# Regrouping the float16 correction matmuls of a fused convolution and feed-forward kernel: one block of sixteen per four steps instead of one of eight per two

## The chip, the cores and the metric

The kernel runs on one core of one Trainium2 chip. The metric is the device time of one execution in microseconds (us). TensorE does the matmuls (PE in the rows; its weight loads are PEld), VectorE (DVE) and ScalarE (ACT) do the elementwise work, GpSimd (POOL) and SyncE (SP) issue transfers.

## The reference

A dynamic convolution with softmax weights over seven taps, then a feed-forward layer with a squared ReLU, over 32768 rows of 192:

```python
w = softmax(weight_gen, axis=-1)                      # (8, 4096, 8 heads, 7 taps)
x = einsum('bshk,bskhg->bshg', w, windows_of(x_pad))  # (32768, 192) after the reshape
h = x @ w_in                                          # (192, 2048)
g = np.maximum(h, 0.0) ** 2
out = g @ w_out                                       # (2048, 192), float32
```

## The kernel before

The rows are cut into 64 chunks of 512. Chunk `c` goes through eight steps `j`, and each step makes two blocks of 128 of the 2048 hidden columns. Float32 accuracy comes from splitting each number into a high part and a rest, so a product is made of several matmuls.

A step of the main loop writes, for PE: first `mm1(c, j)` (L537), 18 matmuls that multiply the chunk's input by `W` into two PSUM banks `ph`: six with `xh` (the input's high part, three pieces of two), six with `xl` (its rest, three pieces of two), six with `xh` again. Then the second product of the step that lies two steps back (`LAG`): `mm2_scaled(c2, j2)`, twelve matmuls with `gh` and `V` at L618. So the second products of a chunk's steps 6 and 7 stand in the next chunk's steps 0 and 1. All these use half of the array's rows each and run in pairs.

For chunks 6 to 62 the rest of `g`, called `gl`, is kept in float16 (five tiles of the pool, and three places inside the tile `du`; `V16`, the float16 weights, lies in `du` too). Its products with `V16` stand in two places of `mm2_scaled`: 32 small ones at L627, all in the chunk's last second product (`j2` = 7), and 32 at L635, four for each step. The line that this case is about says when those at L635 are written: before, in every second step, for that step and the one before it. Nothing reads the sums `acc` before the chunk's last one.

ACT makes from `ph` the ReLU (L554), the square (L561) and the cast to `gh` (L565); DVE makes `gl` (L574) one step later in its own order. When a chunk's last second product is done, `sum_turned` copies two accumulators out on ACT (L668) and adds two on DVE (L670): first `acc2` and `acc3`, which L627 ends, then, after the two casts of the step, `acc0` and `acc1`, which L635 ends.

Between these, DVE makes the convolution of the chunk after next, and the rest `xl` of the next chunk's input, three pieces at L447: two in step 6, the third in step 7. It is read by `mm1` of the next chunk's step 0. In every even chunk from 4 to 60 ACT also measures the next group's inputs in step 2 (`measure`, L279).

The order on each engine is the order in which the program writes it (a manual schedule); there is no planner that weighs costs.

Of the kernel before, what the change touches and what calls it, by code (L numbers as in the profile page):

```python
# [30 lines left out]
def kernel(  # L31
# [81 lines left out]
    def two_halves(t):  # L113
        return t.rearrange("p (i m) -> p m i", i=2)
# [493 lines left out]
    def mm2_scaled(c, j):  # L608
        if j == 0:
            accs[c] = [ps_o.tile([P, N], F32, name=f"acc{t}") for t in range(4)]  # L610
        acc, last = accs[c], j == NJ - 1
        gs = [ghs.pop((c, 2 * j + i)) for i in range(2)]

        def whole(i, b, e):
            fb = 2 * j + i
            for h in range(2):
                rows = slice(h * D1, (h + 1) * D1)
                nc.tensor.matmul(acc[b + h], V[rows, fb, e:e + P], two_halves(gs[i][rows]), start=fb == 0 and e < 2 * P, stop=False)  # L618

        for i, b, e in [(i, 2, P) for i in range(2)] + [(i, 0, e) for i in range(2) for e in (0, 2 * P)]:  # L620
            whole(i, b, e)
        if last:
            for k in range(NJ):
                for h in range(2):
                    for i in range(2):
                        rows = slice(h * D1, (h + 1) * D1)
                        nc.tensor.matmul(  # L627
                            acc[2 + h][i * D1:(i + 1) * D1], V16[rows, 2 * k + i, P:D], gls[c, k][rows, i],
                            start=False, stop=k == NJ - 1, tile_position=(h * D1, i * D1),
                        )  # L630
        for k in (j - 1, j) if j % 2 else ():
            for i in range(2):
                for h in range(2):
                    rows = slice(h * D1, (h + 1) * D1)
                    nc.tensor.matmul(acc[h], V16[rows, 2 * k + i, 0:P], gls[c, k][rows, i], start=False, stop=k == NJ - 1 and i == 1)  # L635
        if last:
            for k in range(NJ):
                del gls[c, k]

    def mm2_turned(c, fb):  # L640
        if is_scaled(c):
            if fb % 2 == 0:
                mm2_scaled(c, fb // 2)
            return
        if fb == 0:
            accs[c] = [ps_o.tile([P, N], F32, name=f"acc{t}") for t in range(4)]
        gh, gl = ghs.pop((c, fb)), gls.pop((c, fb))
        j, i = divmod(fb, 2)
        first, last = fb == 0, fb == NF - 1
        A, B = [(0, 0, gh), (0, 0, gl), (0, 1, gh)], [(2, None, gh), (2, None, gl)]  # L650
        seq = B + A if last or first else A + B
        for n, (b, q, g) in enumerate(seq):
            k = sum(1 for m in seq[:n] if m[0] == b)
            for h in range(2):
                rows = slice(h * D1, (h + 1) * D1)
                w = V[rows, fb, P:2 * P] if q is None else V[rows, fb, 2 * P * q:2 * P * q + P]
                fl = dict(start=first and k == 0, stop=last and k == (2 if b == 0 else 1))
                nc.tensor.matmul(accs[c][b + h], w, (two_halves if is_turned(c) else two_streams)(g[rows]), **fl)  # L658
# [346 lines left out]
```

## Time and profile before

| | |
|---|---|
| median of 3 runs | 2046.72 us (2046.34 to 2046.79) |
| the profiled execution, its own time | 2046.86 us |
| its span, first to last instruction | 2045.1 us |
| PE busy | 2038.0 us, 100% of the span |
| DVE busy | 1873.8 us, 92% |
| ACT busy | 1836.8 us, 90% |
| granted TensorE clock | 1.0 |

The profiled execution is 0.14 us above the median, and 1.76 us of its time lie around the span. Busy time counts instructions under way. Matmuls overlap, so a busy PE need not be at its peak; what matters is how far apart the matmuls start.

### The profile page before, as it was taken

To read this page: it belongs to the slowest core of one execution; us is meant where nothing else is said; L and a number is where in the kernel's file an instruction comes from. 1 tells how busy PE (TensorE), PEld (TensorE's weight loads), DVE (VectorE), ACT (ScalarE), POOL (GpSimd) and SP (SyncE) were. 2 spreads that over 40 slices of the span, in tenths; PEclk is the share of its full clock that TensorE was granted. 3 is DMA by queue.
4 is the path that set the end of the run, shared out by engine and by line. 5 is a ranking of instruction groups with operands and counts; after the bars stand their busy time and mean duration, and the time that the engine had idled before them with its cause. 6 is when DMAs were issued, how large, how long until landed. Compare 5 with 4: busy or idle time off the path is not lost.

```text
span 2045.1 us, 49783 instructions
## 1 busy us (share of the span) xinstructions
PE 2038.0 (100%) x19484; PEld 1637.7 (80%) x19484; DVE 1873.8 (92%) x3009; ACT 1836.8 (90%) x3551; POOL 226.5 (11%) x371
## 2 busy tenths in 40 slices
PE   9999999999999999999999999999999999999999
PEld 8888887877777877777777778787777787877778
DVE  8999999999999999999999999999999999999985
ACT  8989998989989989889899899998898998999986
POOL 0100111011110111101111101111011111011110
PEclk9999999999999999999999999999999999999999
DMA  8433453433444434534345344344453453443422
GB/s 232 92 82 69 97 108 85 104 77 90 105 99 95 93 76 100 111 88 104 71 93 109 93 99 81 84 105 107 92 105 67 95 112 87 103 78 89 105 57 46
DMA packets 346341, 193.44 MB, mean 95 GB/s; under 512 B 216032, under 2 KB 320992, under 8 KB 342264
## 3 DMA queue, kind: packets, MB, share of 16 engines
q1 hardware_dynamic: 324136, 156.00, 32.4%
q0 software_dynamic: 21968, 34.25, 10.2%
q8 instruction: 152, 2.49, 0.5%
q14 instruction: 85, 0.70, 0.1%
HBM read 57.77 MB, written 25.17 MB: 41 GB/s over the span
## 4 chain that ended last, share of the span: by engine, by line
PE 94%; DVE 3%; ACT 1%; DMA 0%; issue 0%; DVEq 0%; SPq 0%
PE ph L537 46%; PE acc L618 28%; PE acc L635 10%; PE acc L627 5%; PE acc L658 3%; PE acc L595 1%; DVE pr L401 0%; DVE gl L577 0%; DVE pr L414 0%; DVE gl L574 0%; DMA pr<-pr 0%; ACT rg L561 0%; DVE xl L447 0%; ACT rg L554 0%; DVE xr L507 0%
## 5 line engine op out<-in xcount | busy, mean ns | idle before, releaser
L537 PE MATMUL ph<-xh,W 64*128 64x512 f32 x6096 | 868.9, 390 | 0.0
L618 PE MATMUL acc<-gh,V 64*128 64x512 f32 x5472 | 665.1, 376 | 0.0
L537 PEld LDWEIGHTS ph<-xh,W 64*128 64x128 f32 x6096 | 580.3, 186 | 101.6 <-DVE W L239 0.3
L554 ACT ACTIVATE rg<-ph 128x512 f32<-128x512 f32 x992 | 541.7, 603 | 123.1 <-PE ph L537 115.1
L561 ACT ACTIVATE rg<-rg 128x512 f32<-128x512 f32 x1007 | 583.9, 640 | 0.2
L565 ACT CAST gh<-rg 128x512 fp32r<-128x512 f32 x1008 | 578.7, 631 | 3.0 <-PE acc L595 3.0
L618 PEld LDWEIGHTS acc<-gh,V 64*128 64x128 f32 x5472 | 518.0, 186 | 72.5
L537 PE MATMUL ph<-xl,W 64*128 64x512 f32 x3048 | 415.1, 376 | 1.1 <-DVE xl L447 0.8
L401 DVE TENSOR_TENSOR pr<-xt,wt 128x768 f32<-128x768 f32 x440 | 412.3, 949 | 2.3
L574 DVE TENSOR_TENSOR gl<-rg,gh 128x512 f16<-128x512 f32 x570 | 388.7, 737 | 2.1 <-ACT gh L565 2.1
L537 PEld LDWEIGHTS ph<-xl,W 64*128 64x128 f32 x3048 | 290.5, 186 | 42.6 <-DVE xl L447 2.1
L414 DVE TENSOR_TENSOR pr<-pr 128x768 f32<-128x768 f32 x309 | 294.3, 952 | 4.2
L574 DVE TENSOR_TENSOR du<-rg,gh 128x512 f16<-128x512 f32 x342 | 231.3, 730 | 4.0 <-ACT gh L565 4.0
L670 DVE TENSOR_TENSOR raw<-acc,raw 128x512 f32<-128x512 f32 x124 | 85.3, 691 | 123.3 <-ACT raw L668 123.3
L672 POOL DMA_DIRECT2D raw<-raw x62 | 51.6, 832 | 1141.0 <-DVE raw L670 1103.8
L635 PEld LDWEIGHTS <-du 64*128 64x128 f16 x1824 | 70.8, 95 | 118.1 <-issue 64.5
L635 PE MATMUL acc<-gl,du 64*128 64x512 f16 x1140 | 152.8, 379 | 0.0
L668 ACT COPY raw<-acc 128x512 f32<-128x512 f32 x124 | 72.1, 587 | 60.3 <-PE acc L627 60.3
L294 POOL DMA_DIRECT2D x_out<-x_fac x232 | 112.0, 491 | 110.1 <-DVE x_fac L291 104.3
L447 DVE TENSOR_TENSOR xl<-xT,xh 128x512 fp32r<-128x512 f32 x186 | 120.8, 679 | 2.8 <-ACT xh L444 2.8
L419 POOL DMA_DIRECT2D pr<-pr x63 | 57.1, 906 | 496.6 <-DVE pr L401 362.3
L444 ACT CAST xh<-xT 128x512 fp32r<-128x512 f32 x186 | 110.1, 636 | 0.4 <-issue 0.3
(129 smaller groups left out, 1267.4 us busy)
## 6 DMA issues: line engine op xcount, KB each, us to landing
xT<-xr SPq DMA_DIRECT2D x496, 96.0 KB
xt<-in_x_dram SPq DMA_DIRECT2D x30, 1344.0 KB
out_dram<-o_sb SPq DMA_DIRECT2D x254, 96.0 KB
pr<-pr POOLq DMA_DIRECT2D x63, 384.0 KB, 4.9
o_sb<-raw SPq DMA_DIRECT2D x372, 64.0 KB
raw<-raw POOLq DMA_DIRECT2D x62, 128.0 KB, 4.9
wt<-in_weight_gen_dram SPq DMA_DIRECT2D x31, 224.0 KB
x_out<-x_fac POOLq DMA_DIRECT2D x232, 0.1 KB, 2.1
```

The source lines that it names most:

```text
L294: nc.gpsimd.dma_start(out=fo[b * P // n:(b + 1) * P // n], in_=f[b::n])
L401: tt(out=dst, in0=src, in1=wf[:, t0 * H:t1 * H, k:k + 1].broadcast_to([P, m, G]), op=ALU.mult)
L414: tt(out=prs[k0], in0=prs[k0], in1=prs.pop(k), op=ALU.add)
L444: nc.scalar.copy(parts["h"][:, k, n], src[k][:, n])
L447: tt(out=parts["l"][:, k, n], in0=src[k][:, n], in1=parts["h"][:, k, n].bitcast(F32), op=ALU.subtract)
L537: nc.tensor.matmul(two[i], w, order(xx[rows, k]), start=(n == 0), stop=(n == last))
L554: nc.scalar.activation(r, ph, AF.Relu)
L561: nc.scalar.activation(r, r, AF.Square)
L565: nc.scalar.copy(gh, rgs[c, fb])
L574: nc.vector.tensor_tensor(out=gl, in0=g, in1=h, op=ALU.subtract)
L618: nc.tensor.matmul(acc[b + h], V[rows, fb, e:e + P], two_halves(gs[i][rows]), start=fb == 0 and e < 2 * P, stop=False)
L635: nc.tensor.matmul(acc[h], V16[rows, 2 * k + i, 0:P], gls[c, k][rows, i], start=False, stop=k == NJ - 1 and i == 1)
```

## The change

The 32 matmuls at L635 of a chunk are written in two blocks of sixteen (for steps 0 to 3 in the second product of step 3, for steps 4 to 7 in that of step 7) instead of four blocks of eight.

```diff
--- before.py
+++ after.py
@@ -628,7 +628,7 @@
                             acc[2 + h][i * D1:(i + 1) * D1], V16[rows, 2 * k + i, P:D], gls[c, k][rows, i],
                             start=False, stop=k == NJ - 1, tile_position=(h * D1, i * D1),
                         )
-        for k in (j - 1, j) if j % 2 else ():
+        for k in range(j - 3, j + 1) if j % 4 == 3 else ():
             for i in range(2):
                 for h in range(2):
                     rows = slice(h * D1, (h + 1) * D1)
```

No instruction is added or removed, and the orders of DVE, ACT, POOL and SP stay as they were. On PE two places move in each of the 57 chunks. The first is the end of a chunk's step 7, here chunk 6 (the second product of its step 5). `acc_3384` and `acc_3385` are its `acc0` and `acc1`; the L537 rows behind are `mm1` of chunk 7, step 0.

```order
@@ -1171,20 +1171,4 @@
 L618 MATMUL acc_3384<-gh,V 128x512
 L618 MATMUL acc_3385<-gh,V 128x512
-L635 LDWEIGHTS du
-L635 MATMUL acc_3384<-gl,du 128x512
-L635 LDWEIGHTS du
-L635 MATMUL acc_3385<-gl,du 128x512
...
 L537 MATMUL ph<-xh,W 128x512 x6
 L537 MATMUL ph<-xl,W 128x512 x6
```

The eight float16 matmuls that stood ahead of the next chunk's first `mm1` are gone from there. The same happens at the end of the chunk's step 3. The second place is the second product of the chunk's step 7, in the next chunk's step 1, behind the 32 at L627 (`acc_3387` is `acc3`).

```order
@@ -1282,4 +1266,20 @@
 L627 MATMUL acc_3387<-du 64x512
 L635 LDWEIGHTS du
+L635 MATMUL acc_3384<-gl,du 128x512
+L635 LDWEIGHTS du
+L635 MATMUL acc_3385<-gl,du 128x512
+L635 LDWEIGHTS du
...
```

They have come here, ahead of the eight of steps 6 and 7. So those for steps 4 and 5 now stand behind L627, and the L627 block has eight fewer matmuls ahead of it in the chunk's order. In the same way the block of step 3 grows to sixteen.

## Rows read from the trace of the kernel before

**Rows 1.** The page: its span, then each engine's busy time and instructions.
```profile
span 2045.1 us, 49783 instructions
PE 2038.0 (100%) x19484; PEld 1637.7 (80%) x19484; DVE 1873.8 (92%) x3009; ACT 1836.8 (90%) x3551; POOL 226.5 (11%) x371
```

**Rows 2.** PE in order of time: start, us, what, [idle before]; chunks 30 and 31.
```profile
986.29 1.46 PE L618 MATMUL acc<-gh,V 64*128 64x512 f32 x12
...
989.52 1.46 PE L618 MATMUL acc<-gh,V 64*128 64x512 f32 x12
...
993.64 1.46 PE L618 MATMUL acc<-gh,V 64*128 64x512 f32 x12
...
1006.72 0.82 PE L627 MATMUL acc<-du 64*64 64x512 f16 x12
1007.47 1.04 PE L635 MATMUL acc<-du 64*128 64x512 f16 x8
```

**Rows 3.** Weight loads waited for, from 240 us: us in total, times, longest.
```profile
PEld ph L537 <- DVE xl L447: 1.2, 1, 1.2
```

**Rows 4.** Weight loads in order of time, chunk 31, step 0.
```profile
999.49 0.62 PEld L537 LDWEIGHTS ph<-xl,W 64*128 64x128 f32 x6
```

**Rows 5.** DVE in order of time, chunk 30.
```profile
978.38 0.69 DVE L670 TENSOR_TENSOR raw<-acc,raw 128x512 f32<-128x512 f32 x1 [0.83 <-ACT raw L668]
...
983.70 1.32 DVE L574 TENSOR_TENSOR gl<-rg,gh 128x512 f16<-128x512 f32 x2
...
999.03 0.68 DVE L447 TENSOR_TENSOR xl<-xT,xh 128x512 fp32r<-128x512 f32 x1
```

**Rows 6.** ACT in order of time, chunk 30, steps 1 to 4.
```profile
976.25 0.59 ACT L668 COPY raw<-acc 128x512 f32<-128x512 f32 x1 [1.05 <-PE acc L627]
...
977.77 0.58 ACT L668 COPY raw<-acc 128x512 f32<-128x512 f32 x1
979.13 1.08 ACT L554 ACTIVATE rg<-ph 128x512 f32<-128x512 f32 x2 [0.78 <-PE ph L537]
...
981.14 1.48 ACT L279 ACTIVATE du<-xt 128x1536 bf16<-128x1536 f32 x1
...
982.88 1.14 ACT L565 CAST gh<-rg 128x512 fp32r<-128x512 f32 x2
...
985.91 0.63 ACT L565 CAST gh<-rg 128x512 fp32r<-128x512 f32 x1
```

**Rows 7.** PE, weight loads and DVE in order of time: chunk 6 ends.
```profile
246.08 0.59 PE L537 MATMUL ph<-xl,W 64*128 64x512 f32 x4
...
247.81 0.81 PE L537 MATMUL ph<-xh,W 64*128 64x512 f32 x6
...
247.49 0.19 PEld L537 LDWEIGHTS ph<-xl,W 64*128 64x128 f32 x2 [1.22 <-DVE xl L447]
...
246.77 0.67 DVE L447 TENSOR_TENSOR xl<-xT,xh 128x512 fp32r<-128x512 f32 x1
```

**Rows 8.** DVE and weight loads in order of time: chunks 8 and 60 end.
```profile
309.16 0.68 DVE L447 TENSOR_TENSOR xl<-xT,xh 128x512 fp32r<-128x512 f32 x1
...
309.66 0.62 PEld L537 LDWEIGHTS ph<-xl,W 64*128 64x128 f32 x6
...
1939.72 0.69 DVE L447 TENSOR_TENSOR xl<-xT,xh 128x512 fp32r<-128x512 f32 x1
...
1940.15 0.62 PEld L537 LDWEIGHTS ph<-xl,W 64*128 64x128 f32 x6
```

**Rows 9.** ACT, DVE and weight loads in order of time: chunk 31 ends.
```profile
1027.71 1.15 ACT L565 CAST gh<-rg 128x512 fp32r<-128x512 f32 x2
...
1028.62 1.35 DVE L574 TENSOR_TENSOR du<-rg,gh 128x512 f16<-128x512 f32 x2
1029.87 0.67 DVE L447 TENSOR_TENSOR xl<-xT,xh 128x512 fp32r<-128x512 f32 x1
...
1030.84 0.62 PEld L537 LDWEIGHTS ph<-xl,W 64*128 64x128 f32 x6
```

## The prediction, made before the changed kernel was run

> **What bounds the kernel now.** I read the page first: PE is busy for 2038.0 of 2045.1 us, DVE for 92% and ACT for 90% [rows 1]. A busy PE proves little, since matmuls overlap, so next I read PE in order of time. From one block at L618 to the next a step takes 989.52 - 986.29 = 3.23 us, for 30 matmuls; the next, which also holds eight at L635, takes 993.64 - 989.52 = 4.12 us for 38 [rows 2]. That is 0.108 us a matmul in both, with the same spacing from the first to the last: PE runs without a gap. Then the table of waits: from 240 us, where the float16 chunks start, PE's weight loads wait only once for another engine, 1.2 us for `xl` [rows 3]. So PE's own stream sets the end, every PE stall adds to the time, and anything else must first make PE wait. The last thing to read is therefore how late PE's inputs come, and only where PE will now arrive earlier.
>
> **What the change takes away.** A block of eight costs 4.12 - 3.23 = 0.88 to 0.89 us; eight matmuls at 0.108 are 0.864. What is left, about 0.016 us, is the price of going from float32 to float16 and back; with rows rounded to 0.01 us it lies between 0 and 0.03. Two of a chunk's five such entries vanish (steps 1 and 5), in 57 chunks: 114 x 0.016 = 1.8 us gained, at most 3.4, at least 0. The matmuls themselves are all still there.
>
> **What it moves.** PE comes 0.88 us earlier to everything between the old and the new place of the eight: from the end of a chunk's step 3 to its step 5, and from the end of its step 7 to the next chunk's step 1. Behind the block of sixteen it is back where it was. The first stretch looks harmless: it takes ReLU banks and casts that were ready long before (the ReLUs at 979.13 end at 980.21 [rows 6], and PE takes their banks again two steps on, in the 1.94 us of 18 matmuls ahead of 986.29 [rows 2], over 4 us later). The second stretch begins with `mm1` of the next chunk, and there DVE is just in time:
>
> - In chunk 30 the third piece of `xl` is done at 999.03 + 0.68 = 999.71 [rows 5]. The loads for `xl` start at 999.49, six in 0.62 us, so the third pair, which waits for it, stands at 999.49 + 2 x 0.216 = 999.92 [rows 4]. The margin is 0.21 us. In the first and the last of the 27 even chunks from 8 to 60 it is 310.09 - 309.84 = 0.25 and 1940.58 - 1940.41 = 0.17 [rows 8].
> - At the end of an odd chunk, 31, it is 1030.84 + 0.43 - 1030.54 = 0.73 [rows 9]. The even ones are later because ACT measures there for 1.48 us [rows 6], and DVE has small operations to add.
>
> Coming 0.88 us earlier eats 0.21 four times over. What a wait there costs is seen once in this trace, at the end of chunk 6: the piece is done at 246.77 + 0.67 = 247.44, the load starts at 247.49, so 0.05 us pass between; the load had waited some 1.2 us, and from the first `xl` matmul to the `xh` matmuls behind it 247.81 - 246.08 = 1.73 us went by where three pairs take 0.65. PE lost 1.08 us of 1.19: some 0.11 us of a wait are free, since a load stands a little ahead of its turn [rows 7].
>
> The Trainium skill, TensorE: Matmul & The Clock Gate, Part 3 (Packing small matmuls), says that PE pulls weight loads ahead of matmuls under way when their row groups do not conflict; taken alone, the loads and matmuls behind the waiting one could fill the gap, and the sum would be the 1.8 us gain of the rival without a wait, below. The rows go against it: in the 1.22 us no other load ran.
>
> **DVE's head start.** DVE's pace is coupled to PE once a chunk, when it waits for ACT's copies (0.83 us before the second add [rows 5]). L627 will now end 0.88 us earlier, so ACT, idle 1.05 us before its first copy, starts it and the two casts 0.88 earlier. The second copy follows the casts today; L635 ended (like 1007.47 + 1.04 = 1008.51 [rows 2], a chunk later) some 0.6 us before it, so it can move 0.55 forward before it waits for the sixteen. DVE would then be 0.55 us ahead. But it can't keep that in an even chunk. Its pair at 983.70 [rows 5] needs the first cast at 982.88, which ends 0.63 later, at 983.51, and 0.05 for the release: it can start at 983.56, only 0.14 earlier. That cast hangs on ReLUs that waited for PE at 979.13, an unmoved matmul, and on the measuring in between [rows 6]; it won't come earlier. Behind it DVE works without a pause up to `xl`. I take 0.13; the ends are 0 and 0.55.
>
> In an odd chunk that pair has no measuring ahead of it, and the tightest is the one at 1028.62, whose cast ends at 1027.71 + 0.63 = 1028.34: 0.23 us of head start remain [rows 9]. There the load would wait 0.88 - (0.73 - 0.05) - 0.23 < 0: nothing.
>
> **The sum.** Per even chunk from 8 to 60: 0.88 - (0.21 - 0.05) - 0.13 = 0.59 us of waiting, less 0.11 = 0.48 us lost; 27 x 0.48 = 13.0 us. Chunk 6, which waits already and whose sums give DVE no head start, loses the full 0.88. Less 1.8 us for the entries: 13.0 + 0.9 - 1.8 = +12.1 us. On the profiled execution's 2046.86 that is 2059.0 us (0.14 less beside the median). The loss is not given back: after the stall ACT and DVE are ahead, but the next chunk's start is set by PE again, and the next even chunk repeats it.
>
> **Rivals.**
>
> *DVE keeps the whole head start* (the cast at 982.88 comes earlier). Wait 0.88 - 0.16 - 0.55 = 0.17, lost 0.06: 27 x 0.06 + 0.9 - 1.8 = +0.7, 2047.6 us. Against it: the ReLUs at 979.13 wait for an unmoved matmul [rows 6].
>
> *No wait at all*: only the entries go, 2046.86 - 1.8 = 2045.1 us. For it: DVE has 8% idle [rows 1]. Against it: that idle time lies ahead of the adds, where it doesn't help `xl`, and chunk 6 shows PE stopping for just this piece.
>
> *No head start anywhere*, because ACT or DVE is slower than I think: the even chunks lose 0.61 us (16.5), the odd ones 0.88 - 0.68 - 0.11 = 0.09 (2.4): +18.0, 2064.9 us.
>
> *Faster*: an entry into float16 is dearer than its matmuls' starts show. The dearest entry here is L618 to L627, and L627 to L635: L627's twelve last start at 1006.72 and L635 at 1007.47, 0.75 us for twelve that run four at a time, 0.054 each, 0.65 [rows 2], so 0.1 us. At that price 114 entries are 11.4 us, and without stalls the time is 2035 us. It beats no change from 0.036 us an entry without stalls, and from 0.16 with them; the rows say 0.016. The Trainium skill, TensorEngine Tiling (Array Packing), Key Properties, says that a change of the tiling mode drains the engine; by that rule L627 pays and an entry that stays at 64 by 128 doesn't, and the trace agrees.
>
> **How the numbers follow.** About 0.2% (4 us) is what a measurement of this kernel can tell from no change. Stalls in the even chunks with a small head start: 0.80, 2055 to 2063 us by itself. Whole head start: 0.06. No wait: 0.06. No head start: 0.05. Dear entries: 0.03. So slower by over 0.2% has 0.85, within 0.2% has 0.12, faster has 0.03. I predict 2059.0 us, with a range from 2048 (just above the whole head start) to 2064 (into the last slow case).
>
> **What would show it.** In the table of waits, weight loads of L537 for `xl` at L447: 28 times instead of once, some 18 us in total (27 x 0.59 + 2.1), on the third pair of a step 0 after an even chunk, none after an odd one. In PE's order of time two plain steps of 3.23 us follow each other everywhere, and the steps with sixteen take 4.95 us or more. DVE's waits before the adds shrink for the second one, and a new wait for L565 of about 0.4 us stands before an L574 pair in even chunks. The granted clock stays at 1.0, as it did through the stall of chunk 6's end. I am wrong if these waits are missing or short, if odd chunks have them too, or if the float16 matmuls inside a block of sixteen don't start 0.108 us apart.

## The result, and the profile after

The changed kernel takes 2060.52 us (median of 6 runs, 2060.1 to 2064.25) where the kernel before, beside it, takes 2046.61: 13.9 us more, a ratio of 1.007 with a 95% interval of 1.0059 to 1.0081. The prediction was 2059.0, slower. Its profiled execution took 2060.67 us.

The page's head, as in [rows 1]:

```profile
span 2058.9 us, 49783 instructions
PE 2043.5 (99%) x19484; PEld 1644.6 (80%) x19484; DVE 1880.2 (91%) x3009; ACT 1840.4 (89%) x3551; POOL 226.4 (11%) x371
```

The span is 13.8 us longer and PE's busy time only 5.5: the same instructions, with gaps between them. The table of waits of the weight loads from 240 us, as in [rows 3], names the gap:

```profile
PEld ph L537 <- DVE xl L447: 20.7, 28, 2.2
```

One wait of 1.2 us has become 28, the longest 2.2 (chunk 6) and the other 27 together 18.5, 0.69 each. PE in order of time, for the same chunk 30 as in [rows 2]; the chunk as a whole comes 5.92 us later here, as the ReLU of its step 2 shows further down:

```profile
994.57 1.46 PE L618 MATMUL acc<-gh,V 64*128 64x512 f32 x12
995.87 1.90 PE L635 MATMUL acc<-gl,du 64*128 64x512 f16 x16
...
999.55 1.46 PE L618 MATMUL acc<-gh,V 64*128 64x512 f32 x12
...
1002.79 1.46 PE L618 MATMUL acc<-gh,V 64*128 64x512 f32 x12
...
1004.73 0.59 PE L537 MATMUL ph<-xl,W 64*128 64x512 f32 x4
1005.62 0.48 PE L537 MATMUL ph<-xl,W 64*128 64x512 f32 x2 [0.29 <-DVE xl L447]
1005.94 0.81 PE L537 MATMUL ph<-xh,W 64*128 64x512 f32 x6
```

The step with sixteen takes 999.55 - 994.57 = 4.98 us, the plain one 3.24. Of the 1.74 us between them sixteen matmuls at 0.108 are 1.73, so one entry costs about 0.01 us, as far as rows rounded to 0.01 can tell. Then the next chunk's first product stops at its third `xl` pair: 1005.94 - 1004.73 = 1.21 us for three pairs that take 0.65, so 0.56 us are lost. The weight loads at that place, as in [rows 4]:

```profile
1004.51 0.41 PEld L537 LDWEIGHTS ph<-xl,W 64*128 64x128 f32 x4
1005.61 0.19 PEld L537 LDWEIGHTS ph<-xl,W 64*128 64x128 f32 x2 [0.69 <-DVE xl L447]
1005.72 0.62 PEld L537 LDWEIGHTS ph<-xh,W 64*128 64x128 f32 x6
```

The third pair would have stood at 1004.51 + 0.43 = 1004.94 and starts at 1005.61, 0.67 us late. DVE in the same chunk, as in [rows 5], with its first add:

```profile
981.92 0.69 DVE L670 TENSOR_TENSOR raw<-acc,raw 128x512 f32<-128x512 f32 x1 [0.84 <-ACT raw L668]
983.73 0.69 DVE L670 TENSOR_TENSOR raw<-acc,raw 128x512 f32<-128x512 f32 x1 [1.11 <-ACT raw L668]
...
989.45 1.38 DVE L574 TENSOR_TENSOR gl<-rg,gh 128x512 f16<-128x512 f32 x2 [0.34 <-ACT gh L565]
...
1004.89 0.67 DVE L447 TENSOR_TENSOR xl<-xT,xh 128x512 fp32r<-128x512 f32 x1
```

And ACT, as in [rows 6]:

```profile
981.30 0.58 ACT L668 COPY raw<-acc 128x512 f32<-128x512 f32 x1 [1.05 <-PE acc L627]
...
983.11 0.58 ACT L668 COPY raw<-acc 128x512 f32<-128x512 f32 x1 [0.19 <-PE acc L635]
985.05 1.08 ACT L554 ACTIVATE rg<-ph 128x512 f32<-128x512 f32 x2 [1.36 <-PE ph L537]
...
988.81 1.13 ACT L565 CAST gh<-rg 128x512 fp32r<-128x512 f32 x2
```

Read from the ReLU: it waits for an unmoved matmul, at 979.13 before and 985.05 now, so 5.92 us is the offset for the chunk. Against it the second copy is 977.77 + 5.92 - 983.11 = 0.58 us earlier and the second add 978.38 + 5.92 - 983.73 = 0.57. The head start is there. Nine instructions later it is used up: the L574 pair waits 0.34 us for a cast that is as late as ever (982.88 + 5.92 = 988.80, now 988.81), and starts only 0.17 earlier. The third piece of `xl` ends 999.71 + 5.92 - 1005.56 = 0.07 us earlier, where PE wanted it 0.88 earlier.

At the end of the odd chunk 31, weight loads and DVE, as in [rows 9]:

```profile
1036.40 0.62 PEld L537 LDWEIGHTS ph<-xl,W 64*128 64x128 f32 x6
...
1036.07 0.68 DVE L447 TENSOR_TENSOR xl<-xT,xh 128x512 fp32r<-128x512 f32 x1
```

The piece is done at 1036.75 and its load stands at 1036.83: just in time, with 0.03 us to spare once the 0.05 for the release is taken off.

### The profile page after: what moved, and what is told of

Read it like the earlier page. It is cut to its first block, busy times and chain, and to the rows that moved or that the text cites. A ratio compares the mean times of both kernels' runs of the same rounds, so it can differ in the third digit from the quotient of the medians.

```text
span 2058.9 us, 49783 instructions
## 1 busy us (share of the span) xinstructions
PE 2043.5 (99%) x19484; PEld 1644.6 (80%) x19484; DVE 1880.2 (91%) x3009; ACT 1840.4 (89%) x3551; POOL 226.4 (11%) x371
## 4 chain that ended last, share of the span: by engine, by line
PE 68%; DVE 18%; ACT 5%; DMA 5%; issue 2%; SPq 2%; DVEq 0%; ACTq 0%
PE ph L537 32%; PE acc L618 18%; PE acc L635 8%; PE acc L627 5%; DVE pr L401 5%; DVE gl L574 3%; DMA o_sb<-raw 3%; DVE du L574 3%; PE acc L658 3%; DVE xl L447 2%; ACT du L279 2%; DMA xT<-xr 2%; SPq L513 1%; ACT rg L561 1%; ACT rg L554 1%
## 5 line engine op out<-in xcount | busy, mean ns | idle before, releaser
L537 PE MATMUL ph<-xh,W 64*128 64x512 f32 x6096 | 847.6, 383 | 0.0
L618 PE MATMUL acc<-gh,V 64*128 64x512 f32 x5472 | 665.1, 376 | 0.0
L537 PEld LDWEIGHTS ph<-xh,W 64*128 64x128 f32 x6096 | 580.1, 186 | 90.5 <-DVE W L239 0.3
L618 PEld LDWEIGHTS acc<-gh,V 64*128 64x128 f32 x5472 | 518.0, 186 | 72.5
L537 PE MATMUL ph<-xl,W 64*128 64x512 f32 x3048 | 422.3, 378 | 9.7 <-DVE xl L447 9.5
L574 DVE TENSOR_TENSOR gl<-rg,gh 128x512 f16<-128x512 f32 x570 | 390.4, 740 | 11.4 <-ACT gh L565 11.4
L537 PEld LDWEIGHTS ph<-xl,W 64*128 64x128 f32 x3048 | 290.4, 186 | 61.3 <-DVE xl L447 21.5
L574 DVE TENSOR_TENSOR du<-rg,gh 128x512 f16<-128x512 f32 x342 | 231.8, 732 | 11.7 <-ACT gh L565 11.7
L635 PEld LDWEIGHTS <-du 64*128 64x128 f16 x1824 | 79.7, 94 | 118.0 <-issue 37.1
L635 PE MATMUL acc<-gl,du 64*128 64x512 f16 x1140 | 142.9, 378 | 0.0
```

Of the source, the lines that this page charges most:

```text
L537: nc.tensor.matmul(two[i], w, order(xx[rows, k]), start=(n == 0), stop=(n == last))
L574: nc.vector.tensor_tensor(out=gl, in0=g, in1=h, op=ALU.subtract)
```

## The experiments

Each edit is to the changed kernel unless it says otherwise. Times are medians beside the kernel before in the same set of runs.

| run | us | before | ratio, 95% interval | chunks 7 to 62 in the trace, us |
|---|---|---|---|---|
| kernel before | 2046.72 | | | 1755.91 |
| changed kernel | 2060.52 | 2046.61 | 1.007 (1.0059 to 1.0081) | 1769.12 |
| e1_mid_only | 2045.44 | 2046.21 | 0.9996 (0.9987 to 1.0005) | 1755.03 |
| e2_end_only | 2062.14 | 2046.21 | 1.0078 (1.0065 to 1.0092) | 1769.58 |
| e3_xl_early | 2043.31 | 2046.21 | 0.9987 (0.9978 to 0.9996) | 1754.29 |
| e4_small_measure | 2048.72 | 2046.21 | 1.0011 (1.0002 to 1.002) | 1757.14 |
| e5_half_dose | 2048.33 | 2046.11 | 1.0012 (1.0003 to 1.0021) | 1757.64 |
| e6_all_in_one | 2044.11 | 2046.11 | 0.9987 (0.9978 to 0.9996) | 1753.36 |
| e7_xl_last | 2044.76 | 2046.11 | 0.9993 (0.9984 to 1.0002) | 1754.28 |
| e9_early_alone | 2045.53 | 2046.11 | 0.9995 (0.9986 to 1.0004) | 1755.91 |
| e10_all_but_first | 2042.93 | 2046.51 | 0.9983 (0.9974 to 0.9992) | 1753.36 |
| e3_again | 2043.70 | 2046.51 | 0.9985 (0.9976 to 0.9994) | 1754.29 |

The last column is read from PE in order of time, in the one profiled execution of each run: from the first matmul of chunk 7's step 2 to the first of chunk 63's step 2. All float16 matmuls of the 56 chunks 7 to 62 lie between them, whatever their grouping. In the kernel before the two are:

```profile
255.63 1.00 PE L537 MATMUL ph<-xh,W 64*128 64x512 f32 x6
...
2011.54 1.00 PE L537 MATMUL ph<-xh,W 64*128 64x512 f32 x6
```

The two executions with e3's kernel agree there to 0.01 us, while PE reached chunk 6 after 214.0 to 218.9 us in these traces, before the regrouping plays any part. So the column tells differences that the intervals of the medians can't.

The theory is that of the prediction: PE comes 0.88 us earlier to a first product whose third `xl` piece is not earlier. The rival is that regrouping costs by itself, in PE's own stream.

**Which of the two moves loses the time.**

```diff
-        for k in range(j - 3, j + 1) if j % 4 == 3 else ():
+        for k in {3: range(4), 5: (4, 5), 7: (6, 7)}.get(j, ()):              # e1_mid_only
+        for k in {1: (0, 1), 3: (2, 3), 7: range(4, 8)}.get(j, ()):           # e2_end_only
```

> Only the block of step 1 moves, into a block of sixteen in step 3; the eight of step 5 stay ahead of the next chunk. Theory (the third xl piece comes too late for a first product that now starts 0.88 us earlier): no first product moves, so no wait for L447 beyond the one of chunk 6; 57 entries into float16 fewer, 57 x 0.015 = 0.9 us less than the kernel before, about 2046. Rival (a block of sixteen costs by itself, wherever it stands): half of the 13.9 us, about 2053.5.

> Only the block of step 5 moves, into the one of step 7; steps 1 and 3 stay as before. Theory: the whole loss stays, 27 waits of about 0.67 us plus chunk 6, and one saved entry a chunk less: 13.9 + 0.9 = 14.8 us over the kernel before, about 2061.5. Rival (the loss comes from blocks of sixteen): half, about 2053.5.

e1 is 0.8 us below the kernel before, within its interval, with the one wait of chunk 6 alone (1.4 us); in the last column it is 0.88 below. e2 is 15.9 above, where 14.8 was expected, with 28 waits, 20.3 us. Of the difference to the changed kernel most is start: its profiled execution, the longest of four, reached chunk 6 at 218.90 us and the changed kernel's at 214.79. In the last column it is 13.7 above the kernel before and the changed kernel 13.2. So the move in the middle of a chunk is harmless and the one at its end loses everything; a block of sixteen costs nothing by itself.

**Half the dose.**

```diff
+        for k in {3: range(4), 5: (4,), 7: (5, 6, 7)}.get(j, ()):
```

> As the changed kernel, but only four of the eight matmuls of step 5 leave it (those of its second half), and go to step 7, which then holds twelve. PE comes 0.45 us earlier to the next chunk instead of 0.88. Theory (a wait of 0.67 us of which 0.11 is free): wait 0.67 - 0.45 = 0.22, lost 0.11, 27 times 3.0 us, chunk 6 0.45 us more, one entry a chunk less, 0.9: 2.5 us over the kernel before, 2048 to 2050. Rival (a loss in proportion to what is moved): half of e2_end_only's loss less the entry of step 1, some 6.5 us, 2053.

2.2 us above the kernel before, not 6.5. The waits are still 28, but shorter; the table of waits, then the weight loads and PE at the end of chunk 30:

```profile
PEld ph L537 <- DVE xl L447: 8.0, 28, 1.8
...
999.22 0.41 PEld L537 LDWEIGHTS ph<-xl,W 64*128 64x128 f32 x4
999.83 0.18 PEld L537 LDWEIGHTS ph<-xl,W 64*128 64x128 f32 x2 [0.21 <-DVE xl L447]
...
999.43 0.88 PE L537 MATMUL ph<-xl,W 64*128 64x512 f32 x6
1000.15 0.81 PE L537 MATMUL ph<-xh,W 64*128 64x512 f32 x6
```

The load is 999.83 - (999.22 + 0.43) = 0.18 us late, and the three pairs take 1000.15 - 999.43 = 0.72 us instead of 0.65: 0.07 lost. The loss is what goes beyond a margin, not a share of what is moved.

**When PE needs the piece.** The six matmuls with `xl` go last in the first product; DVE and ACT keep their order.

```diff
-                mm1(c, j)
+                mm1(c, j, (0, 1, 2, 6, 7, 8, 3, 4, 5), 5) if j == 0 and is_scaled(c) else mm1(c, j)
```

> The changed kernel; in the first product of a scaled chunk's step 0 the six matmuls with xl stand last instead of in the middle, so their third pair comes 0.65 us later. Nothing moves on DVE or ACT. Theory: the wait falls from 0.67 to 0.02 us, within the free 0.11, and chunk 6 waits 0.65 less than with the change: the entries' gain of 1.7 less 0.2, 2044.5 to 2045.5. Rival (PE loses the time in the next chunk's steps anyway, for instance because ACT gets the step's banks no earlier): above 2050.

As expected: 1.35 us below the kernel before (1.63 in the last column), and one wait of 1.6 us, chunk 6's. Here nothing changed but PE's own order by 0.65 us, and the loss is gone, so it was this wait and nothing behind it.

**When DVE has the piece.** The third cast and the third piece come with the first two.

```diff
-                at(m - 1, NJ - 3 + k // 2, f)
-                at(m - 1, NJ - 2 + k // 2, g)
+                at(m - 1, NJ - 3, f)
+                at(m - 1, NJ - 2, g)
```

> The changed kernel with the third piece of xh cast with the first two and the third piece of xl made right behind the first two, one L401 and one L574 pair (2.2 us) earlier on DVE. Theory: the waits for L447 go, the one of chunk 6 too or nearly; left is the gain of the entries, 1.7 us, and up to 1.1 us of chunk 6: 2044 to 2045.2, faster than both. Rival (the loss lies in PE's own stream, or ACT falls behind and the waits only move to another input): no better than 2055.

> The kernel before, in four blocks of eight, with the third piece of xl made early as in e3_xl_early. Theory: it had one wait for xl from chunk 6 on, which cost 1.08 us; that goes and no more: 2045.0 to 2045.6, and e3_xl_early is faster by the entries' 1.7 us. Rival (e3_xl_early is fast because of the earlier piece itself, not of the entries): 2043.5.

e9 is the same edit on the kernel before. e3 is faster than the changed kernel, and faster than the kernel before by 2.9 and 2.8 us in its two sets; 1.7 for the entries and up to 1.1 for chunk 6 were expected, so it came in 0.7 us below its 2044. e9 is 0.6 below the kernel before, within its interval. DVE and the weight loads of e3 at the end of chunk 30:

```profile
992.95 1.89 DVE L447 TENSOR_TENSOR xl<-xT,xh 128x512 fp32r<-128x512 f32 x3
...
995.92 0.62 PEld L537 LDWEIGHTS ph<-xl,W 64*128 64x128 f32 x6
```

All three pieces are done at 994.84, 1.5 us ahead of the third pair's load at 996.35. With the piece in time, only the gain of the regrouping is left: e3 against e9 is the entries, 1.7 us expected. The two differences to the kernel before give 2.3, but their intervals overlap. The last column settles it: 1755.91 - 1754.29 = 1.62, while e9 gains nothing there, so e3 isn't fast because of the earlier piece itself.

**Why DVE cannot be earlier.** L279 measures 96 values of a row instead of all 1536 (work left out: the scaling comes from a part of the inputs). This version has one line more, so its L280 is L279, and so on.

```diff
+            m = min(n, 96)
-            nc.scalar.activation(scrap[:, 0:n], x_tiles[gi][:, r0:r1, :].rearrange("p r d -> p (r d)"), AF.Square, accum_out=x_sum[k])
+            nc.scalar.activation(scrap[:, 0:m], x_tiles[gi][:, r0:r1, :].rearrange("p r d -> p (r d)")[:, 0:m], AF.Square, accum_out=x_sum[k])
```

> The changed kernel, but L279 measures only the first 96 of the values in each row of the group (work left out: the power of two that scales the inputs comes from a part of them). Theory (in an even chunk DVE's head start is cut off by the cast that stands behind the measuring): ACT reaches that cast 1.3 us earlier, DVE keeps most of its 0.55 us, the wait falls from 0.67 to 0.2 or 0.3, the loss from 0.54 to 0.1 or 0.2 a chunk: 2 to 4 us over the kernel before, 2049 to 2051. Rival (the head start is lost elsewhere on DVE, or there is none): 2058 to 2061, as with the change.

2.5 us above the kernel before (1.2 in the last column), as the theory has it. The waits, then DVE and the weight loads in chunk 30:

```profile
PEld ph L538 <- DVE xl L448: 8.8, 28, 2.3
...
984.17 1.35 DVE L575 TENSOR_TENSOR gl<-rg,gh 128x512 f16<-128x512 f32 x2
...
999.63 0.68 DVE L448 TENSOR_TENSOR xl<-xT,xh 128x512 fp32r<-128x512 f32 x1
...
1000.36 0.19 PEld L538 LDWEIGHTS ph<-xl,W 64*128 64x128 f32 x2 [0.30 <-DVE xl L448]
```

The pair of L574 no longer waits, and the wait for `xl` falls from 0.69 to 0.30 here. So the cast behind the measuring is what used up the head start; it isn't all of the wait, since 0.88 is more than margin and head start together.

**One block a chunk.** All 32 in step 7, with both remedies; then the same with chunk 6 left in two blocks.

```diff
+        for k in range(NJ) if last else ():                                   # e6_all_in_one
+        for k in (range(NJ) if last else ()) if c > FIRST else range(j - 3, j + 1) if j % 4 == 3 else ():   # e10_all_but_first
```

> All 32 float16 matmuls of L635 in one block in step 7, with the third xl piece made early and the six matmuls with xl last in the first product of step 0. Theory (nothing else of PE's inputs is closer than 2.6 us, which is how much earlier PE comes now): one entry fewer than e3_xl_early, 0.9 us less, 2042 to 2043. Rival (ACT and DVE cannot follow seven steps of 3.24 us in a row, and PE waits for casts, ReLU banks or the first two xl pieces): 2046 or more.

> As e6_all_in_one, but chunk 6, the first with float16 pairs, keeps the two blocks of sixteen. Theory (e6_all_in_one lost its third entry's gain to 1.1 us of waits in chunk 6 alone, where DVE and ACT are still behind): those waits go, 56 entries of 0.016 us fewer than e3_again on the same chip, 0.9 us less: 2042.2 to 2042.8 where e3_again has 2043.3. Rival (one block in step 7 costs something in every chunk that the waits don't show): no faster than e3_again.

> The kernel of e3_xl_early again, beside e10_all_but_first: 2043.3 us, as then.

e6 missed its 2042 to 2043. Its weight loads' waits up to 260 us, which is into chunk 7:

```profile
PEld ph L537 <- DVE xl L447: 1.5, 4, 0.4
PEld acc L658 <- DVE gl L577: 1.4, 3, 0.6
PEld acc L618 <- ACT gh L565: 0.8, 2, 0.4
```

The row for L618 is new: in chunk 6 PE, 2.6 us early, waits for casts, and again for `xl`. From chunk 6's first matmul to chunk 7's step 2 e6 takes 40.48 us and e3_xl_early 39.36. From there on PE waits no more, so ACT and DVE can follow seven plain steps in a row, and e6 gains what was expected: 1754.29 - 1753.36 = 0.93 us. e10, which spares chunk 6, has none of these waits and is 0.8 us below e3_again beside it, where 0.9 was expected and the rival had nothing. The intervals of the medians overlap, but the last column has the same 0.93. (e10 also asks for `xl` last, which e3_again doesn't; by e7 and e3, 1754.28 and 1754.29, that order alone is worth nothing there.) It is the fastest version, 0.17% below the kernel before.

## Why the prediction was right

**The bound.** PE's stream sets the end, and anything else counts where PE waits: the loss came as gaps in front of one instruction, at L537's third `xl` pair.

**The entries.** Put at 0.016 us each, 1.8 us in all. In the last column e1, which drops one a chunk and touches nothing else, gains 0.88 us for 56, e3 1.62 for 112 and e10 2.55 for 168: 0.0145 to 0.016 each, 1.7 us in all. Right. The prediction gives a chunk five entries; four lead from float32 to float16, since the last block at L635 follows L627, but the two that vanish are counted rightly.

**The margin and the place.** Right, with waits of 20.7 us in all where some 18 were forecast: the third pair of the even chunks' next step 0, 27 times and chunk 6, and none after odd chunks, with 0.03 us to spare as worked out. e2, e7 and e3 show it from three sides.

**The head start.** The mechanism was right, as DVE's and ACT's rows and e4 show. Its size was the term that was off: 0.13 us predicted, 0.07 left at `xl`. The cast freed the pair 0.17 earlier, but the pair took 1.38 us instead of the 1.32 in [rows 5], and some more went on the way; why DVE was slower there wasn't tried. So chunk 30's wait is 0.67 us instead of 0.59 and the loss 0.56 instead of 0.48. Over all 27 it is (13.21 + 1.62) / 27 = 0.55, which makes 1.9 us more than predicted; chunk 6 lost 1.0 instead of 0.9, and the entries gave 0.1 less. That adds up to 12.1 + 2.1 = 14.2 us, which is also what the traces differ by from chunk 6's first matmul to chunk 63's step 2 (1810.56 against 1796.37). Ahead of chunk 6 the changed kernel's execution was 0.4 us shorter, within the scatter of that part, which leaves the 13.8 of the span: by chance the total came out a little closer than its terms.

One sign came out the other way. The wait before the second add was to shrink, and it grew from 0.83 to 1.11 us; it is the first add's that shrank, from 1.54 to 0.84. In the kernel before that add is:

```profile
976.86 0.69 DVE L670 TENSOR_TENSOR raw<-acc,raw 128x512 f32<-128x512 f32 x1 [1.54 <-ACT raw L668]
```

The prediction's own figures say so: the first copy comes 0.88 us earlier and the second only 0.55, so the time between the adds grows.

**The free 0.11 us.** It was worked out from one row and held at two other sizes: 0.67 us late, 0.56 lost, and in e5's chunk 30 0.18 late, 0.07 lost. Over e5's 27 chunks the last column gives (1.73 + 0.88) / 27 = 0.10 lost each, for waits of (8.0 - 1.8) / 27 = 0.23, of which by chunk 30 (0.21 and 0.18) 0.20 is lateness. The rows also show where it comes from: a load stands 1004.73 - 1004.51 = 0.22 us ahead of its matmul. After the wait load and matmul start together, at 1005.61 and 1005.62, and the pair behind follows 1005.94 - 1005.62 = 0.32 us later instead of 0.22. So of the lead of 0.22 us only 0.10 has to be paid, and some 0.11 are free.

**The rivals.** No wait at all, the whole head start and dear entries are excluded by the 28 waits, the L574 wait and the steps' lengths. No head start anywhere is excluded by the second add, 0.57 us earlier, and by the odd chunks, which don't wait. The Trainium skill, TensorE: Matmul & The Clock Gate, Part 3, says that PE pulls weight loads ahead of matmuls under way when their row groups do not conflict. That filled no gap here: in front of the load at 1005.61 no other load ran. The prediction also let matmuls go past the waiting load, which is more than that sentence says.

## What to carry to other kernels

Where an engine runs without gaps, moving its work later makes everything between the two places come earlier on it by the length of what moved. So go through that stretch and list, for each thing it waits for, how long before its turn it is ready now; a margin smaller than the shift is the loss, whatever the move was to save. An engine that is a few per cent idle doesn't help if its idle time lies ahead of another wait, and the remedy is cheap once the late operand is known: make it earlier, or ask for it later. And where a difference is below the scatter of whole executions, compare the time between the same two instructions in their traces.

## What the runs showed of the hardware that was not expected

The wait for `xl`, the moving operand, stands on the weight load, which comes a matmul pair ahead of its own turn. So an operand is wanted 0.22 us before the matmul that reads it (1004.51 and 1004.73); and yet 0.11 us of such a wait cost nothing.

A float16 block between float32 ones at the same tile size costs only about 0.015 us to enter and leave (1.62 us for 112), while the way back from 64 by 64 to 64 by 128 cost about 0.1 us [rows 2]. Chunk 6's stall, 2.2 us at the weight load and 1.8 us of idle PE, left the granted clock at 1.0, the upper of its two levels (2.4 GHz). The window from 245 to 249 us of the changed kernel; its last three columns are PE's clock, the DMA engines' share and GB/s:

```profile
245.00:249.00 4.00, 2.17 (x20) 1.58 (x19) 4.00 (x7) 3.25 (x8) 0.00 (x0) 1.00 0.11 33
```
